# Attention and ELU MLP on one core: subtractions of the inner layer put behind the ELU, other buffers for the first block's outputs, a later first decode, and v scaled on ScalarE at the start

## The chip, the cores and the metric

The kernel runs on one core of one Trainium2 chip. The metric is the device time of one execution in microseconds (us). Three runs of the kernel before the change took 728.32, 730.32 and 732.88 us; the median is 730.32 us.

TensorE is PE in the profile (its weight loads are PEld), VectorE is DVE, ScalarE is ACT, GpSimd is POOL, and SyncE is SP, which here issues all the DMAs.

## The reference: what is computed

All data are float32. An attention block without softmax, with a decaying state, is followed by a two-layer MLP with ELU. There are B = 4 batches, H = 8 heads, S = 768 steps, head size D = 64; the MLP has 3072 tokens, model size 512 and hidden size 2048.

```python
gamma = 1.0 - 2.0 ** (-5.0 - np.arange(H))
for t in range(S):
    state = gamma * state + np.einsum('bhd,bhe->bhde', k[:, :, t], v[:, :, t])
    y[:, :, t] = scale * np.einsum('bhd,bhde->bhe', q[:, :, t], state)
x = y.transpose(0, 2, 1, 3).reshape(B * S, H * D)
h = x @ w_in
g = np.where(h > 0.0, h, np.exp(np.minimum(h, 0.0)) - 1.0)
out = g @ w_out
```

The two weight matrices arrive as float64.

## The kernel before

**Attention.** The tokens are cut into 24 chunks of 128, six to a batch. `scale_v` (line 185) multiplies a chunk's v, in its tile `kvn`, by a power of gamma from the table `vf`; it runs on VectorE for the first four chunks and on GpSimd for the others. `scores` (line 195) forms k times q of all heads in two PSUM tiles `sc`, and VectorE multiplies them with the mask into the tile `pt` (line 207). `values` (line 212) multiplies `pt` with the scaled v into two PSUM tiles `y`, adds this chunk's k times v to a running PSUM tile `kv`, and adds the state of the earlier chunks times q to `y`. VectorE then writes `y` times a table of powers to `xb` (line 252), and ScalarE copies `kv` to the SBUF tile `state` (line 258), which the next chunk uses.

**Decoding the weights.** Each of 16 pieces of the float64 weights is loaded as raw words (`wraw`, three buffers) and made into float32 by `decode` (line 107): ScalarE takes an absolute value (line 124) and converts the low words (line 129), and VectorE runs lines 126, 127, 128 and 130, the last of which writes the result. Pieces 0 to 7 are `w_in` (tiles `w_a`, `w_b`), pieces 8 to 15 are `w_out` (tiles `wo`). Each call also issues the load of a later piece.

**The first block of 512 tokens** takes the plain way. `plain_first` (line 285) makes 16 tiles of the hidden layer: four matmuls into a PSUM tile `hp`, then `elu` (line 277). `elu` puts a Relu and an Exp on ScalarE and leaves its last step on VectorE, line 283, in the list `later`; `flush` (line 273) emits what stands in that list. The flush comes inside the next `elu`, behind that one's two ScalarE instructions. `plain_second` (line 301) runs over the eight pieces of `w_out`: eight matmuls into four PSUM tiles `op`, then four additions and subtractions on VectorE (line 313) for the scheme below, and two DMAs of the piece and its combinations to a scratch tensor in DRAM. Between these pieces stand one `decode` each, the attention of the next four chunks, and `combine_w_in` (line 328) after every second piece. At the end the four `op` tiles are copied to tiles `ot` and sent out (lines 323 to 326). `ot` comes from the pool `hpool`, which has four buffers.

**The other five blocks** use a scheme of seven products for a 2 x 2 block product (Strassen's, in Winograd's form), `strassen` (line 350). The inner layer, `first` (line 378), runs it for four units n = 0 to 3. In one unit product 1 goes to the PSUM tile pa and is copied to SBUF by `kept` (line 342, ScalarE, tile `m`); product 2 goes to pb, and `plus` (line 347, VectorE, tile `h`) adds the copy to it, which gives C11; product 6 is added to pa and kept as u2; product 7 goes to pd; product 5 is added to pa, so it must wait until u2 has been copied; then follow u4 and C22, and behind the "gap" product 3 (C12, read by `elu` straight from pa) and product 4 (C21). Units overlap: products 3 and 4 of unit n are issued behind products 1 and 2 of unit n + 1 and ahead of its products 6, 7 and 5. So TensorE's order is 1, 2, [3, 4 of the unit before], 6, 7, 5. All these matmuls are line 390.

When C12 of a unit has been made, `use` (line 395) flushes the list at once and emits two subtractions (line 403): T3 = C22 - C12 and T1 = C12 - C11. The outer layer, `second` (line 421), reads T1 and T3 in its products 5 and 7 and in the additions of line 439. Its matmuls are line 427, their weights are fetched back from the scratch tensor. The attention of the next four chunks is issued between its products.

The order of work on each engine is that of the program text: the schedule is manual, and each engine takes its instructions in turn. Each f32 matmul of the text stands in the trace as two records.

Of the kernel before, what the change touches and what calls it, by code (L numbers as in the profile page):

```python
# [16 lines left out]
def kernel(  # L17
# [24 lines left out]
    nc = tc.nc  # L42
# [142 lines left out]
    def scale_v(m):  # L185
        if m >= NCHUNK:
            return
        i = chunks[m][1]
        qk, kv = raw[m]
        eng = nc.vector if m < CPB else nc.gpsimd  # L190
        eng.tensor_tensor(  # L191
            out=kv[:, 1], in0=kv[:, 1], in1=vf[:, i].unsqueeze(2).to_broadcast([C, H, D]), op=ALU.mult
        )
# [107 lines left out]
    def plain_second(gs):  # L301

        ops = [ps_f.tile([P, TB], FP32, name="op", tag="f") for _ in range(4)]
        for f in range(NF):
            wo = decoded[2 * NQ + f]
            for row in range(2):
                for d in range(4):
                    nc.tensor.matmul(  # L308
                        ops[d], lhsT=wo[:, row, d * P : (d + 1) * P], rhs=gs[row * NF + f],
                        start=(f == 0 and row == 0), stop=(f == NF - 1 and row == 1),  # L310
                    )
            so = t4.tile([P, 4, 256], FP32, name="so", tag="t4")
            tt = lambda o, x, y, op: nc.vector.tensor_tensor(out=o, in0=x, in1=y, op=op)
            a11, a21, a12, a22 = (wo[:, r, 256 * d : 256 * d + 256] for r in range(2) for d in range(2))
            tt(so[:, 0], a21, a22, ALU.add)
            tt(so[:, 1], so[:, 0], a11, ALU.subtract)
            tt(so[:, 2], a11, a21, ALU.subtract)
            tt(so[:, 3], a12, so[:, 1], ALU.subtract)
            nc.sync.dma_start(scratch[f, :, 0:1024], wo.rearrange("p a b -> p (a b)"))
            nc.sync.dma_start(scratch[f, :, 1024:2048], so.rearrange("p a b -> p (a b)"))  # L320
            yield
        for d in range(4):
            ot = hpool.tile([P, 2, TH], FP32, name="ot", tag="h")
            eng = (nc.scalar.copy, nc.vector.tensor_copy)[d % 2]
            eng(ot.rearrange("p a b -> p (a b)"), ops[d])
            nc.sync.dma_start(out[0, d // 2, :, :, d % 2, :].rearrange("t p c -> p t c"), ot)
# [51 lines left out]
    def first(n, gq):  # L378
# [16 lines left out]
        def use(name, h):  # L395
            g = gpool.tile([P, 2, TH], FP32, name="g", tag="g")
            flat = lambda x: x.rearrange("p a b -> p (a b)")
            elu(flat(g), flat(h))
            gq[name] = g
            if name == "C12":  # L400

                flush()
                sub = lambda o, x, y: nc.vector.tensor_tensor(out=o, in0=x, in1=y, op=ALU.subtract)  # L403
                t3_ = gpool.tile([P, 2, TH], FP32, name="g", tag="g")
                sub(t3_, gq["C22"], gq["C12"])
                sub(gq["C12"], gq["C12"], gq["C11"])
                gq["T3"], gq["T1"] = t3_, gq["C12"]

        return strassen(product, use, None)

# [44 lines left out]
    for j in range(CPB + 1):  # L455
        if j < CPB:
            scale_v(j)
            scores(j)
        if j > 0:
            values(j - 1, ps_f)  # L460
            if j % 2 == 0:
                decode()
    startup.__exit__(None, None, None)
    gpool = ctx.enter_context(tc.tile_pool(name="gpool", bufs=20))
    gs = {}
    for n, _ in enumerate(plain_first(gs)):
        if n % 2 == 0:
            decode()
        if n == 4:
            load(CPB)  # L470
        if n == 8:
            load(CPB + 1)
# [95 lines left out]
```

## Time and profile before

| | |
|---|---|
| median of three runs | 730.32 us (728.32 to 732.88) |
| the profiled execution | 728.61 us, its span 726.8 us |
| PE busy | 687.1 us, 95% of the span |
| DVE, ACT, POOL busy | 317.0, 208.3, 23.4 us |
| chain that ended last, by engine | PE 68%, DVE 14%, ACT 12%, issue 4%, DMA 2% |
| granted TensorE clock, mean | 0.995 |
| data moved | 93.92 MB, 129 GB/s |

The profile is of one execution. The span runs from its first to its last instruction; 1.8 us of the execution's own time lie outside it. Stages, in the trace's time: the first four chunks until 27.7 us, `plain_first` until 82.8, `plain_second` until 155.2, and then five blocks of some 115 us each, of which the inner layer takes the first 60 or so.

A row of the timeline gives the start in us, the busy time in us, the engine, the line, the operation, what is written and read, and the number of instructions merged into the row; a bracket at the end gives the idle time of the engine just ahead of it and what ended that. The view of waits gives the engine and line that waited, what it waited for, the total in us, the number of times and the longest.

### The profile page before, as it was taken

The page shows a single profiled execution, that of the slowest core. Times are in us where ns is not written, and L with a number is a line of the kernel's source. Part 1 is how long each engine was busy: PE and PEld are TensorE (multiplying, and loading weights), DVE is VectorE, ACT ScalarE, POOL GpSimd, SP SyncE. Part 2 cuts the span into 40 slices and gives each one's busy share as a digit, 9 for nine tenths or more (in the row PEclk, how much of TensorE's full clock was granted, in tenths as well). Part 3 has the DMA queues.
Part 4 walks back from the last instruction along what each step waited for, and adds up shares of the span by engine and source line. Part 5 has one row for each costly group of instructions (what it writes and reads, how often), then busy time and mean ns, then how long its engine had stood idle before and what let it go on. Part 6 is the DMA issues. An engine that isn't in the chain of part 4 may idle for free.

```text
span 726.8 us, 9254 instructions
## 1 busy us (share of the span) xinstructions
PE 687.1 (95%) x3904; PEld 542.2 (75%) x3904; DVE 317.0 (44%) x504; ACT 208.3 (29%) x332; POOL 23.4 (3%) x28
## 2 busy tenths in 40 slices
PE   6899899998999999899999999999999999999997
PEld 5444344467888788788888878788888878877886
DVE  5767788753435204445312453522343620353410
ACT  3456622114530003441001543000443100344200
POOL 0000000100000110000100000010000010000000
PEclk9999999999999999999999999999999999999999
DMA  8546578645014663002665001567100553300251
GB/s 336 185 170 235 173 247 287 243 154 171 1 51 138 197 220 92 0 1 81 224 225 167 0 1 59 174 192 229 44 0 17 171 176 91 127 0 1 74 172 44
DMA packets 51929, 93.92 MB, mean 129 GB/s; under 512 B 2224, under 2 KB 39088, under 8 KB 49840
## 3 DMA queue, kind: packets, MB, share of 16 engines
q1 hardware_dynamic: 51888, 93.33, 38.7%
q8 instruction: 31, 0.51, 0.3%
q14 instruction: 10, 0.08, 0.0%
HBM read 78.64 MB, written 14.68 MB: 128 GB/s over the span
## 4 chain that ended last, share of the span: by engine, by line
PE 68%; DVE 14%; ACT 12%; issue 4%; DMA 2%; SPq 0%; DVEq 0%; ACTq 0%
PE ps L427 34%; PE ps L390 16%; PE op L308 8%; ACT r L280 5%; PE sc L204 4%; DVE h L347 3%; PE y L227 3%; ACT r L281 3%; DVE g L403 2%; DVE g L283 2%; ACT m L342 2%; PE y L247 2%; DVE wc L128 2%; DMA qk<-in_qkv_dram 1%; ACT wc L124 1%
## 5 line engine op out<-in xcount | busy, mean ns | idle before, releaser
L427 PE MATMUL ps<-g,ws 128*128 128x256 f32 x1120 | 248.3, 381 | 0.7 <-ACT m L342 0.7
L427 PEld LDWEIGHTS ps<-g,ws 128*128 128x128 f32 x1120 | 211.1, 190 | 31.6 <-ACT m L342 1.1
L347 DVE TENSOR_TENSOR h<-ps,m 128x512 f32<-128x512 f32 x75 | 51.7, 689 | 228.0 <-ACT m L342 140.4
L342 ACT COPY m<-ps 128x512 f32<-128x512 f32 x75 | 43.3, 577 | 193.5 <-PE ps L427 116.3
L390 PE MATMUL ps<-xt,w_b 128*128 128x256 f32 x320 | 77.3, 384 | 17.3 <-ACT m L342 17.3
L390 PEld LDWEIGHTS ps<-xt,w_b 128*128 128x128 f32 x320 | 59.5, 190 | 31.1 <-ACT m L342 23.7
L390 PE MATMUL ps<-xb,w_a 128*128 128x256 f32 x320 | 72.4, 379 | 0.0
L390 PE MATMUL ps<-xt,w_s 128*128 128x256 f32 x320 | 72.4, 379 | 0.0
L390 PEld LDWEIGHTS ps<-xt,w_s 128*128 128x128 f32 x320 | 60.7, 190 | 8.4 <-issue 0.2
L390 PEld LDWEIGHTS ps<-xb,w_a 128*128 128x128 f32 x320 | 60.7, 190 | 8.4 <-issue 0.2
L280 ACT ACTIVATE r<-h 128x512 f32<-128x512 f32 x60 | 37.8, 630 | 101.3 <-DVE h L347 101.3
L281 ACT ACTIVATE r<-r 128x512 f32<-128x512 f32 x96 | 60.5, 630 | 3.0
L308 PE MATMUL op<-g,wo 128*128 128x512 f32 x128 | 58.9, 613 | 2.4 <-DVE g L283 2.4
L283 DVE SCALAR_TENSOR_TENSOR g<-r,h 128x512 f32<-128x512 f32 x60 | 41.1, 686 | 22.0 <-ACT r L281 22.0
L308 PEld LDWEIGHTS op<-g,wo 128*128 128x128 f32 x128 | 24.2, 194 | 32.1 <-issue 27.8
L204 PE MATMUL sc<-qk 64*128 64x128 f32 x384 | 33.5, 300 | 11.9 <-DMA qk<-in_qkv_dram 6.8
L204 PEld LDWEIGHTS sc<-qk 64*128 64x128 f32 x384 | 28.4, 198 | 19.8 <-DVE xb L252 7.6
L191 POOL TENSOR_TENSOR kvn<-kvn,vf 128x512 f32<-128x512 f32 x20 | 21.9, 1094 | 570.5 <-DMA kvn<-in_qkv_dram 407.2
L207 DVE TENSOR_TENSOR pt<-sc,cmask 128x512 f32<-128x512 f32 x48 | 30.9, 685 | 21.5 <-PE sc L204 21.3
L252 DVE TENSOR_TENSOR xb<-y,etab 128x256 f32<-128x256 f32 x48 | 18.4, 418 | 48.0 <-PE y L247 40.8
L258 ACT ACTIVATE state<-kv 128x256 f32<-128x256 f32 x20 | 7.7, 384 | 105.9 <-PE kv L237 105.9
L390 PE MATMUL ps<-xb,w_s 128*128 128x256 f32 x160 | 37.8, 379 | 0.0
(57 smaller groups left out, 464.3 us busy)
## 6 DMA issues: line engine op xcount, KB each, us to landing
ws<-scratch_dram SPq DMA_DIRECT2D x35, 1024.0 KB, 5.7
wraw<-in_w_dram SPq DMA_DIRECT2D x16, 1024.0 KB, 4.9
qk<-in_qkv_dram SPq DMA_DIRECT2D x24, 512.0 KB, 6.5
kvn<-in_qkv_dram SPq DMA_DIRECT2D x24, 512.0 KB, 7.4
out_dram<-h SPq DMA_DIRECT2D x20, 256.0 KB, 5.8
scratch_dram<-wo SPq DMA_DIRECT2D x8, 512.0 KB, 6.8
scratch_dram<-so SPq DMA_DIRECT2D x8, 512.0 KB, 3.4
out_dram<-ot SPq DMA_DIRECT2D x4, 256.0 KB, 6.7
```

The costliest lines, as they stand in the source:

```text
L191: eng.tensor_tensor(out=kv[:, 1], in0=kv[:, 1], in1=vf[:, i].unsqueeze(2).to_broadcast([C, H, D]), op=ALU.mult)
L204: nc.tensor.matmul(sc[a][:, p, :], lhsT=qk[r, 1, p, :], rhs=qk[r, 0, p, :], start=True, stop=True)
L207: nc.vector.tensor_tensor(out=pt[:, a], in0=sc[a], in1=cmask.unsqueeze(1).to_broadcast([C, HP, C]), op=ALU.mult)
L227: nc.tensor.matmul(y[a][c * D : (c + 1) * D, u, :], lhsT=vn[:, h, :], rhs=pt[:, a, p, :], start=(u == 0), stop=(i == 0), skip_group_check= ...
L280: nc.scalar.activation(r, h, AF.Relu, scale=-1.0)
L281: nc.scalar.activation(r, r, AF.Exp, scale=-1.0)
L283: later.append(lambda: nc.vector.scalar_tensor_tensor(g, r, -1.0, h, ALU.add, ALU.max))
L308: nc.tensor.matmul(ops[d], lhsT=wo[:, row, d * P : (d + 1) * P], rhs=gs[row * NF + f], start=(f == 0 and row == 0), stop=(f == NF - 1 and ...
L342: nc.scalar.copy(m, ps)
L347: nc.vector.tensor_tensor(out=h, in0=ps, in1=m, op=ALU.add)
L390: nc.tensor.matmul(ps[:, fi, :], lhsT=w[:, fi, j2, :], rhs=x[:, j2, :], start=(begin and fi == 0 and j2 == 0), stop=(j2 == 1), skip_group_ ...
L427: nc.tensor.matmul(ps[:, d, :], lhsT=ws[:, f, d * P : (d + 1) * P], rhs=gqs[f // 2][name][:, f % 2, :], start=(begin and f == 0 and d == 0 ...
```

## The change

There are four edits.

1. In the inner layer the flush behind C12 is gone, and the two subtractions are appended to the list `later`. They are then emitted by the flush inside the `elu` of C21, behind the last step of C12's ELU.
2. The tiles `ot` come from the pool `t4` (five buffers, used by `pt`, `wo`, `wc`, `so`) instead of `hpool`.
3. For chunks 1 to 3 `scale_v` issues eight ScalarE instructions, one for each head (128 x 64), with the head's column of `vf` as scale; chunk 0 stays on VectorE.
4. The first `decode` stands behind the masks of chunk 3 instead of behind `values` of chunk 1, and the decode behind the 15th tile of `plain_first` is left out. So nine pieces instead of ten are decoded ahead of `plain_second`, and there each piece is decoded one step later than before.

```diff
@@ scale_v
         qk, kv = raw[m]
+        if 0 < m < CPB:
+            for h in range(H):
+                nc.scalar.activation(kv[:, 1, h, :], kv[:, 1, h, :], AF.Copy, scale=vf[:, i, h : h + 1])
+            return
         eng = nc.vector if m < CPB else nc.gpsimd
@@ plain_second
         for d in range(4):
-            ot = hpool.tile([P, 2, TH], FP32, name="ot", tag="h")
+            ot = t4.tile([P, 2, TH], FP32, name="ot", tag="t4")
@@ use, in first
             if name == "C12":
 
-                flush()
                 sub = lambda o, x, y: nc.vector.tensor_tensor(out=o, in0=x, in1=y, op=ALU.subtract)
                 t3_ = gpool.tile([P, 2, TH], FP32, name="g", tag="g")
-                sub(t3_, gq["C22"], gq["C12"])
-                sub(gq["C12"], gq["C12"], gq["C11"])
                 gq["T3"], gq["T1"] = t3_, gq["C12"]
+                later.append(lambda: sub(t3_, gq["C22"], gq["C12"]))
+                later.append(lambda: sub(gq["C12"], gq["C12"], gq["C11"]))
@@ main program
             scale_v(j)
             scores(j)
         if j > 0:
+            if j == CPB:
+                decode()
             values(j - 1, ps_f)
-            if j % 2 == 0:
-                decode()
+    decode()
     startup.__exit__(None, None, None)
     gpool = ctx.enter_context(tc.tile_pool(name="gpool", bufs=20))
     gs = {}
     for n, _ in enumerate(plain_first(gs)):
-        if n % 2 == 0:
+        if n % 2 == 0 and n < 14:
             decode()
```

Line numbers of the changed kernel are 4 higher behind `scale_v`, and 3 higher from the subtractions (line 403, now 406) on.

**Place 1, the inner layer on VectorE.** These are VectorE's instructions from C22 of one unit to C22 of the next. `h<-ps,m` is `plus`, `g<-r,h` and `g<-r,ps` are the last steps of ELUs (the one that reads `ps` is C12's), `g<-g` are the two subtractions. Before:

```order
L347 TENSOR_TENSOR h<-ps,m 128x512
L283 SCALAR_TENSOR_TENSOR g<-r,h 128x512 x2
L283 SCALAR_TENSOR_TENSOR g<-r,ps 128x512
L403 TENSOR_TENSOR g<-g 128x512 x2
L347 TENSOR_TENSOR h<-ps,m 128x512 x2
L283 SCALAR_TENSOR_TENSOR g<-r,h 128x512
```

and changed:

```order
L351 TENSOR_TENSOR h<-ps,m 128x512
L287 SCALAR_TENSOR_TENSOR g<-r,h 128x512 x2
L351 TENSOR_TENSOR h<-ps,m 128x512
L287 SCALAR_TENSOR_TENSOR g<-r,ps 128x512
L406 TENSOR_TENSOR g<-g 128x512 x2
L351 TENSOR_TENSOR h<-ps,m 128x512
L287 SCALAR_TENSOR_TENSOR g<-r,h 128x512
```

The addition of C21 (the first of the two `plus` behind the subtractions before) now stands ahead of C12's last ELU step and of both subtractions.

**Place 2, the start on VectorE.** The rows from the masks of chunk 2 to the end of the first four chunks; `kvn<-kvn,vf` is `scale_v`, `pt` the masks, `xb` the evictions of `y`. Before:

```order
L191 TENSOR_TENSOR kvn<-kvn,vf 128x512
L207 TENSOR_TENSOR pt<-sc,cmask 128x512 x2
L252 TENSOR_TENSOR xb<-y,etab 128x2x128 x2
L126 TENSOR_SCALAR wc<-wc 128x1024
L127 TENSOR_SCALAR wc<-wc 128x1024
L128 SCALAR_TENSOR_TENSOR wc<-wraw,wc 128x1024
L130 ISA w_a_93<-wc,w_a_93 128x2048
L191 TENSOR_TENSOR kvn<-kvn,vf 128x512
L207 TENSOR_TENSOR pt<-sc,cmask 128x512 x2
L252 TENSOR_TENSOR xb<-y,etab 128x2x128 x4
```

and changed:

```order
L211 TENSOR_TENSOR pt<-sc,cmask 128x512 x2
L256 TENSOR_TENSOR xb<-y,etab 128x2x128 x2
L211 TENSOR_TENSOR pt<-sc,cmask 128x512 x2
L256 TENSOR_TENSOR xb<-y,etab 128x2x128 x2
L126 TENSOR_SCALAR wc<-wc 128x1024
L127 TENSOR_SCALAR wc<-wc 128x1024
L128 SCALAR_TENSOR_TENSOR wc<-wraw,wc 128x1024
L130 ISA w_a_93<-wc,w_a_93 128x2048
L256 TENSOR_TENSOR xb<-y,etab 128x2x128 x2
```

The decode of piece 0 stood ahead of chunk 3's masks and now stands behind them, but ahead of chunk 3's eviction to `xb`. On ScalarE the two instructions of this decode move from behind the second `state` copy to behind the third, and eight narrow `kvn` instructions come ahead of each of the first three `state` copies.

**Place 3, the end of `plain_first` on VectorE.** Here `g<-r,hp` are the last steps of the ELUs, `so` the combinations of the first piece of `w_out`. Before:

```order
L130 ISA wo<-wc,wo 128x2048
L283 SCALAR_TENSOR_TENSOR g<-r,hp 128x512 x2
L126 TENSOR_SCALAR wc<-wc 128x1024
L127 TENSOR_SCALAR wc<-wc 128x1024
L128 SCALAR_TENSOR_TENSOR wc<-wraw,wc 128x1024
L130 ISA wo<-wc,wo 128x2048
L283 SCALAR_TENSOR_TENSOR g<-r,hp 128x512 x2
L313 TENSOR_TENSOR so<-wo 128x256
```

and changed:

```order
L130 ISA wo<-wc,wo 128x2048
L287 SCALAR_TENSOR_TENSOR g<-r,hp 128x512 x4
L317 TENSOR_TENSOR so<-wo 128x256
```

The decode of piece 9 no longer stands between the ELUs of the last four tiles; it follows the combinations of piece 8, and every later decode moves back by one step in the same way.

## The prediction, made before the change was run

> **What bounds the kernel now.** I read the busy line, then PE's waits, then the timelines of PE, ACT and DVE at each place where PE waited. The busy line:
>
> ```profile
> PE 687.1 (95%) x3904; PEld 542.2 (75%) x3904; DVE 317.0 (44%) x504; ACT 208.3 (29%) x332; POOL 23.4 (3%) x28
> ```
>
> PE is the bound, so only its idle time, 39.7 us, can be won. The view of waits for PE (total, times, longest):
>
> ```profile
> PE ps L390 <- ACT m L342: 17.3, 16, 2.5
> ...
> PE y L227 <- DVE pt L207: 3.0, 1, 3.0
> PE op L308 <- DVE g L283: 2.4, 1, 2.4
> ```
>
> The first line is 16 waits in the inner layer, one of 2.5 us and 15 of about 1 us. The edits aim at all three lines. Where a row names a line number, it is that of the kernel before.
>
> **Edit 1, the subtractions.** One unit out of the 15, from PE's timeline: product 4 of the unit before, products 6 and 7, then product 5, which waits, and the next product 5.
>
> ```profile
> 171.95 1.89 PE L390 MATMUL ps<-xt,w_b 128*128 128x256 f32 x8
> 173.68 3.62 PE L390 MATMUL ps<-xt,w_s 128*128 128x256 f32 x16
> ...
> 178.27 1.99 PE L390 MATMUL ps<-xt,w_b 128*128 128x256 f32 x8 [0.98 <-ACT m L342]
> ...
> 191.61 1.99 PE L390 MATMUL ps<-xt,w_b 128*128 128x256 f32 x8 [0.99 <-ACT m L342]
> ```
>
> A product takes 173.68 - 171.95 = 1.73 us, seven take 12.1; from one waiting product 5 to the next pass 13.34 us. So each wait costs 1.25 us (the 0.98 shown, the tail of the last matmul, and a slower first one). Product 5 waits for the copy of u2. What ACT did ahead of that copy:
>
> ```profile
> 173.02 0.63 ACT L281 ACTIVATE r<-r 128x512 f32<-128x512 f32 x1
> 176.45 0.63 ACT L280 ACTIVATE r<-h 128x512 f32<-128x512 f32 x1 [2.81 <-DVE h L347]
> 177.12 0.63 ACT L281 ACTIVATE r<-r 128x512 f32<-128x512 f32 x1
> 177.65 0.57 ACT L342 COPY m<-ps 128x512 f32<-128x512 f32 x1
> ```
>
> The copy stood behind C21's Relu and Exp, and these waited 2.81 us for `h` of C21. DVE:
>
> ```profile
> 173.68 0.69 DVE L283 SCALAR_TENSOR_TENSOR g<-r,ps 128x512 f32<-128x512 f32 x1 [0.46 <-ACT r L281]
> 174.40 1.42 DVE L403 TENSOR_TENSOR g<-g 128x512 f32<-128x512 f32 x2
> 175.74 0.68 DVE L347 TENSOR_TENSOR h<-ps,m 128x512 f32<-128x512 f32 x1
> ```
>
> Product 4, which `h` needs, ended at 171.95 + 1.89 = 173.84, but `h` came at 175.74, behind C12's last step and both subtractions. In the new order it stands ahead of them and can start at about 173.9, 1.84 us earlier. The same chain of 2.53 us (175.74 to 178.27) then lets product 5 go at 176.43, while PE gets there only at 173.68 + 2 x 1.73 = 177.14. The copy itself needs product 6, which ends near 175.6, before ACT comes to it at 175.8. So 0.7 us are to spare and the wait is gone: **15 x 1.25 = 18.8 us**.
>
> What becomes late instead: C12's last step goes from 173.68 to about 174.5 and T1 and T3 follow it. Line 439 reads T3 first, some five microseconds later in the last unit and far later in the others. C12's PSUM tile is held 0.8 us longer, but product 7 of the next unit was given another tile, as the semaphores of the changed program show (it waits for no VectorE step). Bounds: nothing gained, if ACT is late for another reason, to 18.8.
>
> **Edit 2, the buffers.** The one wait of 2.5 us is the first unit of the second block:
>
> ```profile
> 158.76 3.66 PE L390 MATMUL ps<-xt,w_s 128*128 128x256 f32 x16
> 164.94 1.99 PE L390 MATMUL ps<-xt,w_b 128*128 128x256 f32 x8 [2.52 <-ACT m L342]
> ...
> 159.10 0.68 DVE L263 TENSOR_TENSOR xt<-xb,xt 128x512 f32<-128x512 f32 x1
> 162.40 0.69 DVE L347 TENSOR_TENSOR h<-ps,m 128x512 f32<-128x512 f32 x1 [2.62 <-DMA out_dram<-ot]
> ```
>
> `h` waited for a buffer of `hpool` that an output DMA still read. With `ot` in the other pool `h` follows the subtractions at 159.7, 2.7 us earlier; product 5 could go at 162.24, against 162.2 on PE's side, so of 2.9 us (164.94 - 162.2, and a slower first matmul) about 0.2 is left: **2.7 us**. The new buffers' last users (a piece and combinations sent to scratch) were issued 10 us or more earlier; should one of those transfers be late, the copies wait instead, and the gain falls to nothing.
>
> **Edit 4, the end of the plain layers.**
>
> ```profile
> 82.76 2.74 PE L308 MATMUL op<-g,wo 128*128 128x512 f32 x6
> 87.92 6.25 PE L308 MATMUL op<-g,wo 128*128 128x512 f32 x10 [2.42 <-DVE g L283]
> 94.11 1.16 PE L204 MATMUL sc<-qk 64*128 64x128 f32 x16
> 95.20 7.13 PE L308 MATMUL op<-g,wo 128*128 128x512 f32 x16
> ...
> 86.04 1.23 DVE L130 CUSTOM_DVE_ANT_0 wo<-wc,wo 128x2048 uint16<-128x2048 uint16 x1
> 87.18 1.28 DVE L283 SCALAR_TENSOR_TENSOR g<-r,hp 128x512 f32<-128x512 f32 x2
> ```
>
> The fourth `op` tile needs the PSUM of the 15th `hp`, whose ELU stood behind the decode of piece 9. PE then ran at half its rate for a while: 10 records took 6.25 us where 16 take 7.13, and the window's clock shows it (below). From 82.76 to 94.11, where the next piece's scores begin, pass 11.35 us instead of 7.1. Without that decode the ELU is done before PE asks: 4.3 us won.
>
> But they are given back in part, since each piece is decoded one step later. After the scores DVE must now mask, combine `w_in`, combine the piece at hand and decode the next, all before PE's next piece but with only one piece and one `values` to cover it:
>
> ```profile
> 95.30 1.29 DVE L207 TENSOR_TENSOR pt<-sc,cmask 128x512 f32<-128x512 f32 x2 [1.41 <-PE sc L204]
> ...
> 103.61 1.23 DVE L130 CUSTOM_DVE_ANT_0 wo<-wc,wo 128x2048 uint16<-128x2048 uint16 x1 [0.19 <-ACT wo L129]
> ...
> 104.35 7.13 PE L308 MATMUL op<-g,wo 128*128 128x512 f32 x16
> ...
> 129.34 7.13 PE L308 MATMUL op<-g,wo 128*128 128x512 f32 x16
> ...
> 137.90 7.13 PE L308 MATMUL op<-g,wo 128*128 128x512 f32 x16
> ```
>
> From the masks to the end of that decode DVE takes 104.84 - 95.30 = 9.5 us, and starts 0.1 behind PE's piece. PE comes to the next piece after 104.35 - 95.20 = 9.15 us at the first such place and after 137.90 - 129.34 = 8.56 at the third; the second, with a `values` of medium length, lies between. New waits: 0.5, 0.95 and 1.1 us, **2.6 us** in all; the pieces in between have cover. Net 4.3 - 2.6 = **1.7 us**. Bounds: 4.3 won if DVE has more slack than I see, and if each wait also brings the half rate (1.8 us each, next part) 3.7 lost.
>
> **Edits 3 and 4, the start.**
>
> ```profile
> 19.75 0.67 PE L247 MATMUL y<-qk,state 64*64 64x128 f32 x16
> 23.46 1.89 PE L227 MATMUL y<-pt,kvn 128*64 128x128 f32 x16 [3.04 <-DVE pt L207]
> 27.73 0.70 PE L292 MATMUL hp<-xb,w_a 128*128 128x512 f32 x1 [0.52 <-DVE xb L252]
> ...
> 16.97 1.15 ACT L124 ACTIVATE wc<-wraw 128x1024 f32<-128x1024 f32 x1
> 19.93 0.38 ACT L258 ACTIVATE state<-kv 128x256 f32<-128x256 f32 x1 [0.75 <-PE kv L237]
> ...
> 22.12 0.68 DVE L191 TENSOR_TENSOR kvn<-kvn,vf 128x512 f32<-128x512 f32 x1
> 27.24 0.76 DVE L252 TENSOR_TENSOR xb<-y,etab 128x256 f32<-128x256 f32 x2 [2.58 <-PE y L247]
> ```
>
> Chunk 3's `values` waited 3.04 us for its masks behind the decode. Now they come first, and these matmuls follow at 20.4 and end at about 22.6. But `xb` of chunk 3, and with it the plain layer, stands behind the decode, which itself begins later: ACT gets to it behind the third `state`, at 19.93 + 0.38 = 20.3 instead of 16.97. From there to DVE's next instruction takes 22.12 - 16.97 = 5.15 us, so `xb` at 25.5 and `hp` 0.49 later (27.73 - 27.24), at 26.0: 1.7 us earlier. PE is then idle from 22.6 to 26.0, 3.4 us. After the 3.04 us above, 16 records took 1.89 us instead of 1.09, and granted clocks in these windows (column behind POOL) were low:
>
> ```profile
> 18.00:28.00 10.00, 6.43 (x103) 5.55 (x102) 7.08 (x13) 3.25 (x6) 0.00 (x0) 0.83 0.62 239
> 28.00:60.00 32.00, 32.00 (x75) 14.08 (x75) 23.71 (x28) 18.85 (x26) 1.04 (x1) 1.00 0.50 173
> 83.00:95.00 12.00, 9.58 (x32) 4.04 (x30) 10.21 (x14) 5.08 (x7) 0.00 (x0) 0.86 0.64 190
> ```
>
> The half rate at 87.92 cost 6.25 - 10/16 x 7.1 = 1.8 us. It now falls on the first `hp` tiles: -1.7 + 1.8 = **0.1 us lost**. The 24 narrow ScalarE instructions have no like in the trace; each lies between nothing and 0.38 us (the `state` copy, four times as wide), eight between 0 and 3.0. The nearest row is `state`; I take 2. ACT is idle there (0.75 us ahead of `state`, more elsewhere), and the only one whose cover may fail is chunk 3's, which would hold the third `state` and the decode by up to 1 us.
>
> The Trainium skill, "TensorE: Matmul & The Clock Gate", section "Why this matters for your kernels", asks for no PE idle gap over about 3 us, and its Part 1 gives one idle window as about 3.4 us, in a window that runs freely. The trace disagrees in part: 2.42 us sufficed at 87.92, 2.52 us at 164.94 did not. By the page the 3.4 us are at the edge, so the clock may stay up, which is the third rival.
>
> **Sum.** 18.8 + 2.7 + 1.7 - 0.1 = 23.1. From the profiled span 726.8 that makes 703.7, and with the 1.8 outside it (728.61 - 726.8) 705.5. The runs' median is 1.7 above the profiled execution; on that footing I say **707 us**.
>
> **Rivals.**
> 1. *The wait is only shortened* (7%): u2's copy still stands behind Relu and Exp of C21, and 0.7 us of slack is thin. If half of each stays, 9.4 come back: 716. Against: every step of the chain has its row.
> 2. *Plain layers lose* (8%): the three new waits bring the half rate, 3 x 1.8 = 5.4 more: 712. For: 2.42 us of idleness was enough. Against: the 15 waits of 0.98 show no slower matmuls behind them.
> 3. *No half rate at the start* (12%): 1.8 less, 705. For: after 2.52 us of idleness at 164.94 eight records took 1.99 us, hardly more than the 1.89 of the others. Against: 2.42 and 3.04 us brought it.
> 4. *Slower than before* (2%): PE, now 98% busy, is granted a lower clock. Place: all matmuls, 687 us. It decides below 0.963: 687 x (0.995/0.963 - 1) = 23 us eats the gain; at 0.95 it costs 33, giving 740. Against: 28 to 60 us has PE busy 32.00 of 32.00 at clock 1.00.
> 5. *The buffers don't do it* (2%): `h` waits for something else: 710.
>
> The forecast itself holds 69%. **How the numbers follow**: rivals 2, 3 and 5 lie inside 702 to 713, together with the runs' spread of some 2 us and the bounds of the start and the decodes; what is left out is rivals 1 and 4 and tails, under 2 in 10. A measurement of this kernel can tell about 1%, 7 us, from no change: faster 0.95 (all but rival 4 and the far end of rival 1), same 0.03, slower 0.02.
>
> **What would show it.** Right: no wait of `ps` on `m` in the inner layer above 0.3 us; units of 12.1 us; `h` of C21 within 0.2 us of product 4's end; three waits of PE on a `wo` (line 130) of 0.4 to 1.2 us; `hp` from about 26, at half rate at first. Wrong: product 5 still waiting, product 7 waiting for C12's ELU, or a granted clock under 0.98.

## The result and the profile after

The changed kernel takes 705.44 us (median of four runs, 702.92 to 706.98), against 730.45 us for the kernel before in runs beside it (728.32 to 732.88). The ratio is 0.9653, 95% interval 0.9612 to 0.9695: 3.5% faster, 25.0 us. The forecast was 707. The profiled execution took 705.43 us, its span 703.6. One execution of the experiments, a run of edit 1 alone, had all its matmuls at half rate (16 records of the inner layer in 7.72 us instead of 3.62) and took 1447.37 us; the medians and ratios below leave it out.

TensorE has the same 3904 instructions as before and more of the span, and the chain that ended last is now nearly all PE. From the page of the changed kernel, the busy line and the chain by engine:

```profile
PE 681.0 (97%) x3904; PEld 541.9 (77%) x3904; DVE 314.3 (45%) x501; ACT 213.8 (30%) x356; POOL 24.2 (3%) x28
...
PE 92%; DVE 5%; DMA 1%; issue 0%; SPq 0%; ACT 0%; DVEq 0%; ACTq 0%
```

The chain was 68% PE, 14% DVE and 12% ACT before: the DVE and ACT steps of the inner layer have left it. The view of waits for PE in the changed kernel (total, times, longest):

```profile
PE sc L208 <- DMA qk<-in_qkv_dram: 6.5, 3, 4.7
PE sc L208 <- DVE xb L256: 5.1, 10, 0.5
PE hp L296 <- DVE xb L256: 3.4, 1, 3.4
PE op L312 <- DVE wo L130: 3.0, 3, 1.6
PE ps L430 <- ACT m L346: 0.7, 1, 0.7
```

All 16 waits of `ps` on `m` in the inner layer are gone (the 0.7 belongs to the outer layer, line 430), and so are the waits on `pt` and on `g`. The wait of the first `hp` has grown from 0.5 to 3.4 us, and one line is new: three waits on a decoded `wo`.

**Where the time came from.** Four points on PE's timeline cut the execution into stages: the first `hp`, the first `op`, the first product of the second block, and that block's first product 5. Each number below is the difference of two starts on PE, before and after.

| stage | before, us | after, us | won, measured | won, predicted |
|---|---|---|---|---|
| start to first `op` | 82.76 | 82.16 | 0.60 | -0.1 |
| first `op` to the second block | 155.20 - 82.76 = 72.44 | 153.46 - 82.16 = 71.30 | 1.14 | 1.7 |
| to its first product 5 | 164.94 - 155.20 = 9.74 | 160.51 - 153.46 = 7.05 | 2.69 | 2.7 |
| from there to the end | 726.8 - 164.94 = 561.86 | 703.6 - 160.51 = 543.09 | 18.77 | 18.8 |
| span | 726.8 | 703.6 | 23.2 | 23.1 |

**The inner layer.** PE's timeline of the changed kernel; the first row is the product 5 that waited 2.52 us before, the last row the second product 5 after it (its window ends within it, so only its start counts):

```profile
160.51 1.98 PE L394 MATMUL ps<-xt,w_b 128*128 128x256 f32 x8
...
167.51 1.89 PE L394 MATMUL ps<-xt,w_b 128*128 128x256 f32 x8
...
172.69 1.89 PE L394 MATMUL ps<-xt,w_b 128*128 128x256 f32 x8
...
184.77 1.46 PE L394 MATMUL ps<-xt,w_b 128*128 128x256 f32 x6
```

No row has a bracket, and those left out have none either, so PE did not wait, and a unit takes 184.77 - 172.69 = 12.08 us instead of 13.34. The chain that feeds the product 5 at 172.69, on DVE and then on ACT:

```profile
169.44 0.69 DVE L351 TENSOR_TENSOR h<-ps,m 128x512 f32<-128x512 f32 x1 [0.64 <-PE ps L394]
170.04 0.68 DVE L287 SCALAR_TENSOR_TENSOR g<-r,ps 128x512 f32<-128x512 f32 x1
170.75 1.42 DVE L406 TENSOR_TENSOR g<-g 128x512 f32<-128x512 f32 x2
```

```profile
170.16 0.63 ACT L284 ACTIVATE r<-h 128x512 f32<-128x512 f32 x1 [0.94 <-DVE h L351]
...
171.36 0.56 ACT L346 COPY m<-ps 128x512 f32<-128x512 f32 x1
```

`h` of C21 now waits for PE itself: product 4 ends at 167.51 + 1.89 = 169.40, `h` starts at 169.44. The copy of u2 ends at 171.36 + 0.56 = 171.92, and PE comes to product 5 at 172.69: 0.77 us to spare, where 0.7 had been worked out. C12's last step and the subtractions follow, and nobody waits for them.

**The end of the plain layers**, PE's timeline of the changed kernel:

```profile
82.16 7.03 PE L312 MATMUL op<-g,wo 128*128 128x512 f32 x16
...
99.86 7.13 PE L312 MATMUL op<-g,wo 128*128 128x512 f32 x16 [0.42 <-DVE wo L130]
...
118.37 7.13 PE L312 MATMUL op<-g,wo 128*128 128x512 f32 x16 [1.60 <-DVE wo L130]
...
136.15 7.13 PE L312 MATMUL op<-g,wo 128*128 128x512 f32 x16 [1.01 <-DVE wo L130]
```

The first piece runs through: the next scores begin at 89.12, 6.96 us after 82.16, where 11.35 passed before. The three waits that were forecast stand at the three places, 0.42, 1.60 and 1.01 us (forecast 0.5, 0.95, 1.1), and no matmul behind them is slowed: 7.13 each time.

**The start**, from PE's timeline, and the window over the first `hp` tiles (the column behind POOL is the granted clock):

```profile
21.36 0.67 PE L251 MATMUL y<-qk,state 64*64 64x128 f32 x16
25.46 8.80 PE L296 MATMUL hp<-xb,w_a 128*128 128x512 f32 x16 [3.43 <-DVE xb L256]
```

```profile
21.50:30.00 8.50, 5.07 (x23) 2.31 (x21) 7.68 (x10) 2.80 (x4) 0.00 (x0) 0.80 0.48 145
```

The first `hp` starts 2.27 us earlier than before, and its first 16 records take 8.80 us instead of 7.13: 1.67 us go back to the clock.

### The profile page after: what moved, and what is told of

Read it like the earlier page. It is cut to its first block, busy times and chain, and to the rows that moved or that the text cites. A ratio compares the mean times of both kernels' runs of the same rounds, so it can differ in the third digit from the quotient of the medians.

```text
span 703.6 us, 9258 instructions
## 1 busy us (share of the span) xinstructions
PE 681.0 (97%) x3904; PEld 541.9 (77%) x3904; DVE 314.3 (45%) x501; ACT 213.8 (30%) x356; POOL 24.2 (3%) x28
## 4 chain that ended last, share of the span: by engine, by line
PE 92%; DVE 5%; DMA 1%; issue 0%; SPq 0%; ACT 0%; DVEq 0%; ACTq 0%
PE ps L430 35%; PE ps L394 34%; PE hp L296 8%; PE op L312 5%; PE sc L208 4%; PE y L231 3%; DMA qk<-in_qkv_dram 1%; PE y L251 1%; PE kv L241 1%; DVE w_s L333 1%; DVE wc L128 1%; DVE xb L256 1%; DVE pt L211 1%; DVE so L317 1%; DVE wo L130 1%
## 5 line engine op out<-in xcount | busy, mean ns | idle before, releaser
L394 PE MATMUL ps<-xt,w_b 128*128 128x256 f32 x320 | 75.7, 379 | 0.0
L312 PE MATMUL op<-g,wo 128*128 128x512 f32 x128 | 57.0, 598 | 3.0 <-DVE wo L130 3.0
```

What stands on the lines that cost most here:

```text
L312: nc.tensor.matmul(ops[d], lhsT=wo[:, row, d * P : (d + 1) * P], rhs=gs[row * NF + f], start=(f == 0 and row == 0), stop=(f == NF - 1 and ...
L394: nc.tensor.matmul(ps[:, fi, :], lhsT=w[:, fi, j2, :], rhs=x[:, j2, :], start=(begin and fi == 0 and j2 == 0), stop=(j2 == 1), skip_group_ ...
```

## The experiments

Theory: the time came from two orders. On VectorE, C12's steps stood in the in-order queue ahead of an addition that starts the chain to product 5; and the buffers of the outputs held the same addition once. The plain layers are a small exchange of one wait for three. Rivals: the gain comes from elsewhere (a stage that begins at another time, ScalarE's share of the work), or any order of the subtractions would do as long as one of them moves.

### Edit 1 alone

```diff
@@ use, in first, against the kernel before
-                flush()
                 sub = ...
-                sub(t3_, gq["C22"], gq["C12"])
-                sub(gq["C12"], gq["C12"], gq["C11"])
+                later.append(lambda: sub(t3_, gq["C22"], gq["C12"]))
+                later.append(lambda: sub(gq["C12"], gq["C12"], gq["C11"]))
```

> Edit 1 alone (the two subtractions behind C12's ELU), all else as before. Theory A (the order on VectorE made 15 product 5s wait): the 15 waits of 1 us go, the wait of 2.5 us in the first unit of the second block stays; span 726.8 - 18.8 = 708.0. Rival B (the h tiles wait for buffers that output DMAs hold, so that edit 2 does most of the work): the 15 waits stay near 1 us and the span is above 720.

Measured: 711.28 us (median of three, 709.13 to 711.71) against 730.3, ratio 0.9733 (0.9698 to 0.9767), 19.0 us less. The waits are read from a second profile of the same kernel:

> The kernel before with edit 1 alone, once more, because the first profiled execution of it ran all its matmuls at half rate and its profile shows nothing of the waits. Theory (the 15 waits of product 5 are the cost, and only those): the units are 12.1 us, the 15 waits are gone, the long one of about 2.5 us at the first unit of the second block stays in part (the outputs' buffers are still the old ones), and the span is 726.8 - 18.8 = 708. Rival (part of the 18.8 us comes from the other edits, for instance through a stage that starts at another time): waits of product 5 on m of 0.3 us or more are left and the units are longer than 12.3.

Measured: span 707.5 us, the execution 709.25. PE's timeline of this second run:

```profile
164.32 1.99 PE L390 MATMUL ps<-xt,w_b 128*128 128x256 f32 x8 [2.63 <-ACT m L342]
...
176.51 1.89 PE L390 MATMUL ps<-xt,w_b 128*128 128x256 f32 x8
...
188.60 1.89 PE L390 MATMUL ps<-xt,w_b 128*128 128x256 f32 x8
```

The 15 waits are gone and the sixteenth, for the buffer, stands at 2.63 us. Units take 188.60 - 176.51 = 12.09 us. From the first product 5 to the end pass 707.5 - 164.32 = 543.2 us, what the full change takes (543.1): edit 1 does all of the 18.8 us, without help of the others.

### Edit 1 by half: one subtraction stays ahead

```diff
@@ use, in first, against the changed kernel
-                later.append(lambda: sub(t3_, gq["C22"], gq["C12"]))
+                flush()
+                sub(t3_, gq["C22"], gq["C12"])
                 later.append(lambda: sub(gq["C12"], gq["C12"], gq["C11"]))
```

> The changed kernel with half of edit 1 taken back: the flush and the first of the two subtractions stand ahead of the addition of C21 again, the second subtraction stays behind. Theory (product 5 waits for a chain from the addition of C21 over Relu, Exp and the copy of u2, and TensorE gets there 0.7 us after the chain is through): the addition comes 1.2 us later than in the changed kernel, so the copy ends 0.5 us after TensorE is there; product 5 waits 0.2 to 0.5 us by the profile, a unit takes 12.6 to 12.9 us, and the 15 units cost 7 to 11 us: span 711 to 715, median 713 to 717. Rival 1 (any instruction of C12 ahead of the addition gives the whole wait, since that step waits for ScalarE): units of 13.3, span 722. Rival 2 (the chain has more slack than 0.7 us): no wait, units of 12.1, span 703.6.

Measured: 713.34 us (712.67 to 713.43), ratio 0.9779 (0.9744 to 0.9815), span 710.9. PE and, behind it, DVE and ACT of one unit in this kernel:

```profile
166.81 1.89 PE L394 MATMUL ps<-xt,w_b 128*128 128x256 f32 x8
...
172.42 1.99 PE L394 MATMUL ps<-xt,w_b 128*128 128x256 f32 x8 [0.27 <-ACT m L346]
...
185.04 1.99 PE L394 MATMUL ps<-xt,w_b 128*128 128x256 f32 x8 [0.26 <-ACT m L346]
```

```profile
168.55 0.69 DVE L287 SCALAR_TENSOR_TENSOR g<-r,ps 128x512 f32<-128x512 f32 x1 [0.46 <-ACT r L285]
169.27 0.69 DVE L406 TENSOR_TENSOR g<-g 128x512 f32<-128x512 f32 x1
169.88 0.68 DVE L351 TENSOR_TENSOR h<-ps,m 128x512 f32<-128x512 f32 x1
```

```profile
171.80 0.57 ACT L346 COPY m<-ps 128x512 f32<-128x512 f32 x1
```

The addition comes at 169.88 where product 4 ended at 166.81 + 1.89 = 168.70: 1.2 us late, and the copy ends at 172.37 where PE would have come at 171.99, 0.38 us late. A unit takes 12.62 us, 0.54 more than with nothing ahead, and 15 times that is the 8 us by which the stage grew (710.9 - 159.81 = 551.1, against 543.1). So the slack reads as a threshold: the first 0.77 us of lateness are free, and what goes beyond costs a little more than its size in each unit. Here 0.38 us cost 0.54; before the change the copy ended at 178.22 where PE would have come at 177.14, and 1.08 us cost 13.34 - 12.08 = 1.26. Both rivals, the whole wait and no wait, are out.

### The buffers alone

```diff
@@ plain_second, against the kernel before
-            ot = hpool.tile([P, 2, TH], FP32, name="ot", tag="h")
+            ot = t4.tile([P, 2, TH], FP32, name="ot", tag="t4")
```

> Edit 2 alone (ot in the other pool). Theory A: only the one wait of 2.5 us goes; span 726.8 - 2.7 = 724.1, which the timing can hardly tell from no change. Rival B: the 15 waits go with it, span under 712.

Measured: 726.89 us (724.0 to 727.87), ratio 0.9939 (0.992 to 0.9957). The first line of its waits on PE:

```profile
PE ps L390 <- ACT m L342: 14.8, 15, 1.0
```

The wait of 2.5 us has gone and the 15 others stand. From the second block's first product to its product 5 pass 164.20 - 157.14 = 7.06 us instead of 9.74: 2.7 us, as reckoned. The span of this one execution, 726.1 us, is still only 0.7 below, because its first 16 `hp` records took 9.54 us instead of 7.13 (the last section shows its clock).

### The start and the decodes alone (edits 3 and 4)

```diff
@@ scale_v, against the kernel before
+        if 0 < m < CPB:
+            for h in range(H):
+                nc.scalar.activation(...)
+            return
@@ main program
-            values(j - 1, ps_f)
-            if j % 2 == 0:
-                decode()
+            if j == CPB:
+                decode()
+            values(j - 1, ps_f)
+    decode()
...
-        if n % 2 == 0:
+        if n % 2 == 0 and n < 14:
```

> Edits 3 and 4 alone (v of chunks 1 to 3 on ScalarE, first decode later, nine pieces ahead of the second plain layer). Theory A: first product of the second block about 1.7 us earlier (start 0.6, plain layers 1.1), span about 725.1; three new waits of TensorE on a decoded piece, sum 3.0 us. Rival C (the earlier plain layers have no part in the gain, or it is given back in full by the decodes): span 726.8 within 0.5.

Measured: 728.81 us (724.64 to 730.4), ratio 0.9968 (0.9943 to 0.9993): the two edits are worth 1.5 us in the medians, at the edge of what can be told. The runs fall into two groups: four with a mean granted clock of 1.00 took 724.64 to 725.44 us, the six with 0.993 to 0.998 took 728.04 to 730.4. The profiled execution is of the first group. Its first 16 `hp` records took 7.11 us, so the second block begins 155.20 - 151.60 = 3.6 us earlier than before and not the 1.7 expected. From the first `op` to the second block pass 151.60 - 80.31 = 71.29 us, as with the full change. The waits on `wo` sum up to 3.0 again, and the 16 waits on `m` are all there (17.4 us).

### Edit 3 taken back

```diff
@@ scale_v, against the changed kernel
-        if 0 < m < CPB:
-            for h in range(H):
-                nc.scalar.activation(...)
-            return
```

> The changed kernel without edit 3: v of chunks 1 to 3 scaled on VectorE as before. Theory A: VectorE has room there once the decode stands behind the masks, so edit 3 is worth nothing: first matmul of the plain layer at 25.5 within 0.4, no wait of TensorE for a mask above 0.5 us, span 703.6 within the 2 us that the clock's half rate at the start moves it. Rival E: edit 3 is what brings the masks early; the plain layer starts 1 us or more later.

Measured: 706.84 us (704.73 to 706.97), ratio 0.9679 (0.9645 to 0.9712), which overlaps with the full change. The first `hp` starts at 25.51 instead of 25.46: whether VectorE scales a chunk in 0.68 us or ScalarE in 2.02 (eight instructions), neither stands in the way of the first `hp`. Edit 3 is worth nothing that shows, so the earlier start is the work of edit 4.

### The decode behind the 15th tile put back

```diff
@@ main program, against the changed kernel
-        if n % 2 == 0 and n < 14:
+        if n % 2 == 0:
```

> The changed kernel with the decode behind the 15th tile of the first plain layer put back (ten pieces ahead again). Theory A: the wait of 2.4 us and the half rate behind it come back (4.3 us), the three waits of 3.0 us go; the second plain layer, from its first product to the second block's first, takes 72.4 us instead of 71.3. Rival C: the two cancel, 71.3 within 0.2.

Measured: 707.08 us (706.23 to 708.72), ratio 0.9691 (0.9657 to 0.9725). The old wait is back and the three new ones are gone; PE's timeline of this kernel:

```profile
82.52 2.74 PE L312 MATMUL op<-g,wo 128*128 128x512 f32 x6
87.64 6.25 PE L312 MATMUL op<-g,wo 128*128 128x512 f32 x10 [2.38 <-DVE g L287]
```

From the first `op` to the second block pass 154.93 - 82.52 = 72.41 us instead of 71.30. Leaving that decode out is thus worth 1.1 us, less than the 1.7 predicted.

### combine_w_in behind the decode

The three new waits come from VectorE's queue: masks, `combine_w_in`, the combinations of the piece, then the decode that PE waits for. The combination of `w_in` is not needed soon.

```diff
@@ main program, against the changed kernel
             scores(m)
-            combine_w_in(n // 2)
         else:
+            combine_w_in(n // 2)
             values(m)
```

> The changed kernel with combine_w_in one step later, behind the next decode on VectorE. Theory A (the three waits of 3.0 us in sum come from the four combinations standing ahead of the decode): they vanish and nothing takes their place, span 703.6 - 3.0 = 700.6. Rival D (VectorE is simply full there, so that the wait moves to the next piece or to the scores): waits of the same sum in other places, span 703.6 within 0.5.

Measured: 701.99 us (701.96 to 703.49), ratio 0.9618 (0.9591 to 0.9645). The view of waits for PE in this kernel, without its two lines on `sc`:

```profile
...
PE hp L296 <- DVE xb L256: 3.4, 1, 3.4
PE ps L430 <- ACT m L346: 0.7, 1, 0.7
```

The line on `wo` is gone and nothing has come in its place. From the first `op` to the second block pass 151.54 - 83.48 = 68.06 us, 3.24 less than with the change. So the three waits cost 3.24 us, a little more than the 3.03 that they show, and the whole gain of leaving the decode out (4.4 us) is to be had without giving anything back. The span of this execution, 701.7 us, is 1.1 above the 700.6 expected, because its first 16 `hp` records took 9.90 us and not 8.80; the other three runs have spans of 700.2.

### Why the middle wait was 1.60 us and not 0.95

In the changed kernel one VectorE row of `combine_w_in` ahead of that wait is twice as long as its neighbours, while GpSimd scales a chunk's v. DVE, then POOL, of the changed kernel:

```profile
110.04 1.41 DVE L333 TENSOR_TENSOR w_b<-w_b 128x512 f32<-128x512 f32 x1
111.49 0.69 DVE L333 TENSOR_TENSOR w_s<-w_b,w_a 128x512 f32<-128x512 f32 x1
```

```profile
109.73 1.18 POOL L195 TENSOR_TENSOR kvn<-kvn,vf 128x512 f32<-128x512 f32 x1 [35.69 <-DMA kvn<-in_qkv_dram]
```

The test moves the next four chunks' scaling to ScalarE as well:

```diff
@@ scale_v, against the changed kernel
-        if 0 < m < CPB:
+        if 0 < m < 2 * CPB:
```

> The changed kernel, with the v of the next four chunks too scaled on ScalarE, so that GpSimd has nothing to do during the plain layers. Theory (the middle wait on a decoded piece was 1.6 us and not the 0.95 reckoned because one VectorE instruction of combine_w_in took 1.41 us instead of 0.69 while GpSimd scaled a v): all rows of combine_w_in take 0.69 us, no VectorE row between 84 and 154 us is doubled, the waits are 0.4, 0.9 and 1.0 us, together 2.3, and from the first op to the first product of the next block pass 70.6 us instead of 71.3. Rival 1 (the doubled row is VectorE's own, or comes from a DMA): a row of 1.4 us stands there again and the waits sum up to 3.0. Rival 2 (ScalarE's sixteen microseconds of narrow scales hold up the decodes that stand behind them): a wait on a decoded piece grows beyond 1.7 us, with ScalarE named as what VectorE waited for.

Measured in one execution: 704.48 us, span 702.7. The wait on `wo` in this kernel; then, from its DVE timeline, the second row of `combine_w_in` and the end of a later decode; then POOL:

```profile
PE op L312 <- DVE wo L130: 2.3, 3, 1.0
```

```profile
109.85 0.69 DVE L333 TENSOR_TENSOR w_b<-w_b 128x512 f32<-128x512 f32 x1
...
140.03 1.86 DVE L130 CUSTOM_DVE_ANT_0 wo<-wc,wo 128x2048 uint16<-128x2048 uint16 x1
```

```profile
139.42 1.38 POOL L195 TENSOR_TENSOR kvn<-kvn,vf 128x512 f32<-128x512 f32 x1 [137.26 <-DMA kvn<-in_qkv_dram]
```

The waits are 0.42, 0.87 and 1.01 us, and the stage takes 152.55 - 81.97 = 70.58 us, the 70.6 expected. One point of the expectation was wrong: GpSimd had one scale left in this stretch, of the ninth chunk, at 139.42. It supports the reading, since the one VectorE row that lies across it is the one that is stretched (1.86 instead of 1.23), in a place where nobody waits for it. In the other runs the middle wait went the same way: 1.60 us where a GpSimd scale fell on the second row of `combine_w_in` (edits 3 and 4 alone, 107.61 to 109.06), 0.95 where it ended before (edit 3 taken back, 108.38 to 109.42). In the next experiment's kernel the scale fell on the third place instead (128.54 to 129.58, on a row of 1.42 us at 128.71), and there the middle wait is 0.88 us and the third 1.73. So which wait grows depends on when the scale's data arrive.

### The gap ahead of the plain layers filled, too long

Between the last matmul of the first four chunks and the first `hp`, PE gets matmuls whose result is not used.

```diff
@@ main program, against the changed kernel
     decode()
+    dm = ps_f.tile([C, HP, C], FP32, name="dm", tag="f")
+    for _ in range(6):
+        for p in range(HP):
+            nc.tensor.matmul(dm[:, p, :], lhsT=raw_last[0:D, 1, p, :], rhs=raw_last[0:D, 0, p, :], start=True, stop=True)
     startup.__exit__(None, None, None)
```

> The changed kernel with 24 throw-away matmuls (48 records, about 3.3 us, their result is not used) ahead of the plain layer, in TensorE's idle 3.4 us. If the half rate there comes from the idleness: the first 16 records of the plain layer take 7.1 us instead of 8.8 and never more, start of the plain layer at 25.5, span about 701.8. Rival F (the half rate comes at its own times, whatever TensorE did just before): 8 us or more again.

Measured: 706.06 us (704.81 to 707.5), ratio 0.9675 (0.9641 to 0.9709). PE's timeline of this kernel:

```profile
22.46 5.62 PE L471 MATMUL dm<-qk 64*128 64x128 f32 x48
28.01 7.13 PE L296 MATMUL hp<-xb,w_a 128*128 128x512 f32 x16
```

The rate of `hp` was full again, but the fill had been sized by the scores' 0.07 us a record and took 5.62 / 48 = 0.117. It overran the gap by 2.5 us and ate what it won.

### The gap filled by half as many

```diff
@@ main program, against the kernel with the gap filled
-    for _ in range(6):
+    for _ in range(3):
```

> The changed kernel with 24 throw-away matmul records (half as many as in the filled-gap run, where 48 took 5.6 us and overran the gap of 3.4 us by 2.5) between the last matmul of the first four chunks and the first hp; their result is not used. Theory (it is the idle gap that lets TensorE fall to half rate, and the first attempt lost its gain only by its length): the throw-away records take 2.8 us, 22.0 to 24.9, the first hp starts at 25.5 as in the changed kernel and its first 16 records take 7.1 us instead of 8.8; what follows is 1.7 us earlier, span about 701.9, median about 703.7. Rival 1 (a gap of 0.6 us left behind them, or low load before, lets the rate fall all the same): 16 records take more than 8 us. Rival 2 (VectorE and ScalarE are slowed by the added matmuls or hp is held up by another buffer): the first hp starts later than 25.8.

Measured: 703.01 us (702.56 to 703.97), ratio 0.9644 (0.9602 to 0.9686); 2.4 us below the changed kernel. PE's timeline of this kernel:

```profile
21.52 2.94 PE L471 MATMUL dm<-qk 64*128 64x128 f32 x24
25.03 7.10 PE L296 MATMUL hp<-xb,w_a 128*128 128x512 f32 x16 [0.56 <-DVE xb L256]
```

The first `hp` is not later, and from it to the first `op` pass 80.04 - 25.03 = 55.01 us instead of 56.70 in the changed kernel, which is the 1.7 us of half rate. The span, 700.8 us, is 2.8 below the changed kernel's: besides these 1.7 us the first four chunks ended 0.43 us earlier, and the middle wait was 0.88 us instead of 1.60, so the fill itself is worth 1.7. The idle gap was the cause of the slow first tiles, and not the work that stands there.

### The first decode in steps

The gap itself comes from VectorE: the first decode stands whole between the masks of chunk 3 and the eviction that `hp` waits for. Here its steps are spread over the first chunks, into time in which VectorE waited for PE, on top of the kernel with `combine_w_in` behind the decode.

```diff
@@ main program, against the kernel with combine_w_in behind the decode
             scale_v(j)
             scores(j)
+        if j == 2 or j == 3:
+            next(steps)
         if j > 0:
-            if j == CPB:
-                decode()
             values(j - 1, ps_f)
+        if j == 1:
+            steps = first_decode()
+            next(steps)
+        if j == 2:
+            next(steps)
     decode()
```

`first_decode` holds the instructions of `decode` for piece 0, with a `yield` behind the Abs, behind the first and behind the second VectorE instruction.

> The kernel with combine_w_in behind the decode, and the first decode cut into steps that stand between the masks of chunks 2 and 3, its first ScalarE instruction ahead of chunk 2's v. Theory A: VectorE is done with piece 0 and chunk 3's eviction at about 23.1 instead of 25.4, TensorE idles 1.1 us instead of 3.4 and keeps its rate; span 703.6 - 3.2 (decodes) - 2.3 - 1.8 = 696.3. Rival: VectorE or ScalarE holds up the chunks instead, start of the plain layer no earlier than 25, span 700.

Measured: 698.11 us (697.71 to 698.95), ratio 0.9567 (0.9539 to 0.9596), span 695.9. PE and DVE of this kernel:

```profile
22.66 7.13 PE L316 MATMUL hp<-xb,w_a 128*128 128x512 f32 x16 [0.88 <-DVE xb L276]
```

```profile
17.23 0.68 DVE L145 TENSOR_SCALAR wc<-wc 128x1024 uint32<-128x1024 uint32 x1
17.83 1.28 DVE L231 TENSOR_TENSOR pt<-sc,cmask 128x512 f32<-128x512 f32 x2
...
21.53 1.41 DVE L276 TENSOR_TENSOR xb<-y,etab 128x256 f32<-128x256 f32 x4
```

The masks of chunk 3 come at 17.83 as in the changed kernel (17.89), and two of the four decode steps, at 15.64 and 17.23, are done before them. The first `hp` starts 2.8 us earlier, at full rate, after an idle time of 0.88 us; the first `op` comes at 77.70 instead of 82.16. This is the fastest version: 32.0 us below the kernel before, 7.3 below the changed one.

## Why the prediction was right, point by point

- **Edit 1, 18.8 us:** right in mechanism and size, 18.77. Shown by edit 1 alone (19.0 in the medians, the stage of 543.2 us) and by the half step, whose cost of 0.54 us a unit follows from the slack of 0.77. The first rival, that the wait is only shortened, needed that slack to be smaller than reckoned; it is 0.77 by the trace. Product 7 never waited for C12's last step.
- **Edit 2, 2.7 us:** right, 2.69, and 2.68 alone. The working's 2.9 less 0.2 is loose, since its own times give 164.94 - 162.24 = 2.70, and the slower first matmul that it counted in stayed (1.98 us for the product after, 1.99 before). What was feared of the new buffers (an older transfer that is late) did not come: the rival of 710 is out.
- **Edit 4 at the end of the plain layers, 1.7 us net:** right in mechanism, mis-sized. The gain was 11.35 - 6.96 = 4.4 (predicted 4.3). Given back were 3.2 instead of 2.6, since the middle wait was 1.60 us and not 0.95, which is outside the 0.4 to 1.2 named as a sign of being right. The step that failed took VectorE's `combine_w_in` rows at 0.69 us each, and did not look at what GpSimd does at that time. The trace of the kernel before has such a row too: 1.36 us at 113.81, beside a GpSimd scale that began at 113.58. The rival by which these waits would bring the half rate is out: every piece behind them took 7.13 us.
- **Edits 3 and 4 at the start, 0.1 us lost:** 0.6 won. Reckoned from ScalarE's Abs of the first decode at 19.73, `xb` came at 24.89, after 5.16 us (reckoned: 5.15). But the Abs itself stood at 19.73 and not at 20.3, since the scores at 13.99 came at 13.51 in this execution, 0.48 us earlier, and since the Abs starts 0.28 us behind the start of the `state` copy (19.45) and not 0.38. The 0.48 us are a difference between executions and no gain of the edits. The half rate then cost 1.67 us where 1.8 was taken. That each narrow ScalarE instruction lies in free time was right too; eight take 2.02 us, where 2 was taken between bounds of 0 and 3.0.
- **The third rival, no half rate at the start,** was one of chance: of the seven profiled executions with an idle time of 3.4 us ahead of the first `hp`, one had none (edits 3 and 4 alone, 7.11 us for 16 records), five took 8.64 to 8.80 us and one 9.90. The last section shows which gaps brought it.
- **The granted clock under 0.98** did not come: 0.997, with PE busy 97% of the time.
- **The step from span to median, +1.7 us:** this is the 1.6 us by which 707 lies above 705.44. The sum itself came out at 705.5 for the profiled execution, which took 705.43. The kernel before was profiled in an execution that lay 1.7 below its median, and that was carried over as if it were a property of the kernel. It is one of the execution: with the changed kernel the profiled execution and the median agree within 0.01. The profiled execution had a mean granted clock of 0.995; beside the experiments the runs of the kernel before at 0.995 took 727.5 to 730.4 us, those at 0.991 took 731.24 to 732.77.

The sum of 23.1 against 23.2 is thus better than its terms, and that is luck: the start came out 0.7 us better, most of it by the 0.48 us between executions, and the plain layers 0.6 worse.

## What to carry to other kernels

Where an engine that takes its instructions in order feeds the engine that bounds the kernel, ask of each of its instructions who waits for it, and put those that nobody needs soon (here two subtractions, in an experiment `combine_w_in`) behind the one that starts the chain. Measure the slack first: lateness below it is free, and what goes beyond is paid in each turn of the loop. A step that moves one wait away usually leaves an idle time elsewhere; split the instruction group that stands in it, or fill it, before it costs the clock as well.

## What the runs showed of the hardware

**The half rate after an idle time comes in steps of 3.41 us.** The first rows of the plain layers in three kernels that differ little there, from PE's timeline (the first is with edits 3 and 4 alone, the second with `combine_w_in` behind the decode, the third the kernel before with the other buffers):

```profile
25.30 7.11 PE L296 MATMUL hp<-xb,w_a 128*128 128x512 f32 x16 [3.44 <-DVE xb L256]
```

```profile
25.68 9.90 PE L296 MATMUL hp<-xb,w_a 128*128 128x512 f32 x16 [3.43 <-DVE xb L256]
```

```profile
27.28 9.54 PE L292 MATMUL hp<-xb,w_a 128*128 128x512 f32 x16 [0.51 <-DVE xb L252]
```

After the same 3.4 us of idleness the first 16 records took 7.11 us here, 9.90 there, and 8.80 in the changed kernel. In the third the idle time lay four microseconds earlier (3.05 us, ahead of `values`) and the low rate reached into `hp` all the same. The Trainium skill, "TensorE: Matmul & The Clock Gate", Part 1, gives the low rate as lasting for about 3.4 us, in a window that runs freely, and calls it run-variable. The traces agree with such a window, but the low rate can last several of them: their record of the granted clock has one low stretch of 3.41 us at the start of the changed kernel (26.57 to 29.99), of 6.83 us in the second kernel here, of 10.24 us in the third and none in the first. One stretch of 3.41 us at half rate costs 1.71 us, against the 1.67 seen.

The same record shows what goes with the fall. Cut into stretches of 3.41 us, counted from where the record begins, the changed kernel and, behind it, the kernel with edits 3 and 4 alone look like this (length, then PE's busy time; the column behind POOL is the granted clock):

```profile
23.16:26.57 3.41, 1.11 (x3) 0.66 (x4) 3.23 (x6) 1.14 (x2) 0.00 (x0) 1.00 0.50 159
26.57:29.99 3.42, 3.42 (x5) 1.37 (x5) 2.85 (x3) 0.00 (x0) 0.00 (x0) 0.50 0.64 187
```

```profile
20.28:23.69 3.41, 1.59 (x42) 1.27 (x38) 3.00 (x5) 3.41 (x5) 0.00 (x0) 1.00 0.22 87
23.69:27.10 3.41, 1.80 (x5) 0.87 (x6) 3.34 (x6) 0.42 (x1) 0.00 (x0) 1.00 0.69 269
```

In the first the gap leaves PE busy for 1.11 of 3.41 us, a share of 0.33, and the next stretch is at half rate. In the second a boundary cuts the same gap in two, the shares are 0.47 and 0.53, and the clock stays up. In the 13 traces that have such a record it fell 13 times ahead of the kernel's end, each time behind a stretch with a share of 0.39 or less, and it never fell behind one of 0.44 or more. That also accounts for why 2.42 us were enough at 87.92 in the kernel before (0.99 of 3.41 us busy, 85.03 to 88.44) and 2.52 us at 164.94 were not (a boundary at 163.53; 2.30 and 2.01 busy). No run moved a gap on purpose, so the rule is read from the traces as they fell. As an estimate from these shares, a single idle time below 0.56 x 3.41 = 1.9 us would not bring the half rate here; gaps of 0.56 and 0.88 us, with no long one ahead of them, did not. How long the low rate lasts came out less cleanly: it went on behind shares of 0.65, 0.72 and 0.85 and ended behind one of 0.82. The spread of a kernel's runs goes with the same clock (the groups of edits 3 and 4 alone, and the kernel before above), though only one execution of each was traced.

**GpSimd stretches VectorE.** An addition of 128 x 512 with both inputs in SBUF took 1.41 instead of 0.69 us beside a GpSimd multiplication, and the GpSimd instruction took up to 2.02 us instead of 1.04. The Trainium skill, "SBUF — State Buffer", section "SBUF: two separate sides", has the two share a pair of ports that one of them holds for a whole instruction while the other is blocked. The trace agrees within 0.15 us: GpSimd ended at 109.73 + 1.18 = 110.91, and VectorE's row at 111.45, 0.54 later, most of its own 0.69.

**Matmuls on the same rows of the array, not settled.** The throw-away matmuls (64 x 128) took 0.117 to 0.122 us a record, the scores of the same shape 1.16 / 16 = 0.07. The program has the scores alternate between the two halves of the rows and between two PSUM tiles, and the throw-away ones all use the first half and one tile. Either may be the reason; no run changed one alone.
